# Retention and two MLPs on one core: conversion and retention steps dealt out in slots a step apart, and a pair's load moved behind the step that frees its place

## The chip, the cores and the metric

One core of a Trainium2 chip. TensorE multiplies, VectorE, ScalarE and GpSimd do element work, SP issues most of the DMAs. Each engine runs its own list in the order in which it was written and waits at semaphores. The metric is device time in microseconds of one execution.

## The reference

```python
scores = (q @ k.T) / sqrt(64)                      # 4 batches, 8 heads, 576 positions, 64 wide
ret    = scores * gamma[h] ** (i - j) * (j <= i)   # retention: decay, causal
x      = (ret @ v) -> 2304 tokens x 512
x      = softplus(x @ w_in1) @ w_out1              # d_ff 2048
out    = h * sigmoid(1.702 * h) @ w_out2, h = x @ w_in2
```

The weights come in as 64-bit words.

## The kernel before, in words

The 2304 tokens are worked in five blocks: 512 positions of each of the batches 0 to 3, and a block "t" with the last 64 positions of all four (256 tokens). `order` is 0, 1, 2, t, 3, first through layer 1, then through layer 2. A block has 16 units f, one for each 128 columns of d_ff. A unit is two halves on TensorE: `mm1` (12 matmuls into `ph`) and, two units behind (LAG), `mm2` (12 into the four banks `y`). Every product is made of three, since both operands are split into a high and a low part (`hi` casts, `lo` subtracts). Between the halves ScalarE turns `ph` into g, casts it to gh, and VectorE subtracts to gl (`start`, `split`; `split` runs as `hook` behind the first of mm2's four sub-products).

Everything else of layer 1 is dealt out between the products. `side()` is called twice in mm1 and twice in mm2; each call adds a rate to two counters and for each whole one takes a slot, which is one `next()` of a generator. Two generators are in it:

- `batch(b)`: the retention of the next batch, eight pair-chunks (two heads, 256 positions). `scale_pair` (ScalarE) and `load_pair` (SP, three places `raw`) in one slot, `step` in the next. A step puts out the chunk before (TensorE reads its q and v, so only then is its place free) and makes states `sv`, scores and masked scores `a` of the new one; VectorE does all that follows TensorE in it. Rate 0.31.
- the conversion of weights (`conv`): a tile of words goes through ScalarE (L92), three VectorE instructions (L94, L95, L98), a ScalarE cast and a VectorE subtraction (`lo`, L82), in four slots. In block 0 these are the 16 tiles of layer 1 (`w1_steps`, rate 1.25, and `pre` forces f + 2 tiles ahead of unit f). From block 1 on they are 32 half tiles of layer 2 (`w2_steps`, rate W2RATE), which are read by SP, converted, stored to HBM and loaded again in layer 2; words and results share two places (`raw64`), and what is left of them at block 3's start is done there at once.

Ahead of block 0, `first_batch` runs the first batch's retention alone, with two conversion slots behind each step from the sixth on. At a block's end `done` copies each y bank to one of two `yb` tiles and stores it. At a block's start `pre` empties the retention generator and splits the new x.

## Time and profile before

| what | us |
|---|---|
| time, median of 3 runs (lowest to highest) | 934.18 (933.38 to 937.91) |
| profiled execution | 934.67 |
| its span, first to last instruction | 933.0 |
| TensorE busy | 889.5 (95%) |
| VectorE busy | 407.4 (44%) |
| ScalarE busy | 302.9 (32%) |
| GpSimd busy | 20.3 (2%) |
| granted clock, mean | 0.979 |

Busy times are means over stages that differ. The span is the profiled execution's own; 1.67 us lie around it. PE is TensorE, PEld its weight loads, DVE VectorE, ACT ScalarE, POOL GpSimd, SPq the queue of SP. A releaser behind "<-" is what ended a wait. L82 and L79 / L77 are the lines of the helpers `lo` and `hi`, so their rows are told apart by the names of the tiles.

### The profile page before, as it was taken

What the parts mean: (1) busy time and instruction counts of PE and PEld (TensorE: products, weight loads), DVE (VectorE), ACT (ScalarE), POOL (GpSimd) and SP (SyncE); (2) the same over time, 40 slices, a digit from 0 to 9 for tenths busy, and PEclk for the clock granted to TensorE, in tenths of its full rate; (3) what the DMA queues carried; (4) which work ended last, traced back from release to release, by engine and by line L of the source; (5) the groups of instructions that cost most, each with busy time, mean ns of one, the idle gap of its engine ahead of it and who ended that gap; (6) DMA issues with size and microseconds to landing.
All of it is one profiled execution on the core that took longest, in us unless ns stands there. A gap on an engine that the chain in (4) does not pass through costs nothing.

```text
span 933.0 us, 12052 instructions
## 1 busy us (share of the span) xinstructions
PE 889.5 (95%) x4928; PEld 732.3 (78%) x4928; DVE 407.4 (44%) x759; ACT 302.9 (32%) x541; POOL 20.3 (2%) x41
## 2 busy tenths in 40 slices
PE   9588798999999999989999999999999999999997
PEld 5366577888887778879888888888888888988886
DVE  7877774366666566621211232232223222333222
ACT  3344343334444334422322322232223222333221
POOL 0000000000000000000100110000000000000000
PEclk9799789999999999999999999999999999999999
DMA  9804432245556655420355640001001000200001
GB/s 353 348 1 139 162 114 105 76 172 205 188 181 235 208 210 185 166 109 1 122 208 189 214 148 1 1 31 61 0 1 68 1 1 0 91 2 22 1 1 45
DMA packets 33783, 101.71 MB, mean 109 GB/s; under 512 B 3392, under 2 KB 5440, under 8 KB 31680
## 3 DMA queue, kind: packets, MB, share of 16 engines
q1 hardware_dynamic: 29952, 79.45, 24.1%
q0 software_dynamic: 3776, 21.50, 6.5%
q8 instruction: 38, 0.62, 0.3%
q14 instruction: 17, 0.14, 0.1%
HBM read 74.72 MB, written 26.21 MB: 108 GB/s over the span
## 4 chain that ended last, share of the span: by engine, by line
PE 72%; issue 13%; DVE 7%; DMA 5%; ACT 2%; SPq 0%; POOL 0%; DVEq 0%; ACTq 0%; POOLq 0%
PE ph L111 35%; PE y L111 34%; DMA w_raw<-w_in 2%; PE ps_h L273 2%; DVE wa L98 2%; DVE wa L95 1%; DMA w_kqv<-kqv 1%; DVE w_raw L94 1%; DMA w_raw<-w_out 1%; PE ps_s L304 1%; DVE a L317 1%; ACT wa L92 1%; DVE sv L312 1%; DVE w L82 1%; DMA raw<-kqv 1%
## 5 line engine op out<-in xcount | busy, mean ns | idle before, releaser
L111 PE MATMUL ph<-xh,w 128*128 128x512 f32 (+1 forms) x1280 | 372.6, 376 | 14.1 <-DVE xf L327 6.1
L111 PEld LDWEIGHTS ph<-xh,w 128*128 128x128 f32 x1280 | 236.0, 192 | 60.1 <-issue 6.9
L111 PE MATMUL ph<-xl,w 128*128 128x512 f32 (+1 forms) x640 | 239.7, 375 | 3.4 <-DVE xl L82 3.4
L111 PE MATMUL y<-gh,w 128*128 128x512 f32 (+1 forms) x640 | 198.7, 374 | 5.7 <-DVE yb L79 3.7
L111 PE MATMUL y<-w,gh 128*128 128x512 f32 x576 | 189.5, 389 | 0.0
L82 DVE TENSOR_TENSOR gl<-g,gh 128x512 fp32r<-128x512 f32 (+1 forms) x160 | 102.2, 639 | 183.9 <-ACT gh L77 181.6
L174 DVE TENSOR_TENSOR g<-ph,g 128x512 f32<-128x512 f32 (+1 forms) x80 | 51.0, 638 | 214.3 <-ACT g L167 214.3
L111 PEld LDWEIGHTS ph<-xl,w 128*128 128x128 f32 x640 | 123.2, 192 | 25.6 <-DVE xl L82 4.6
L111 PEld LDWEIGHTS y<-gh,w 128*128 128x128 f32 x640 | 118.6, 191 | 28.7 <-DVE yb L79 4.5
L111 PEld LDWEIGHTS y<-w,gh 128*128 128x128 f32 x576 | 108.1, 188 | 22.0
L111 PE MATMUL y<-gl,w 128*128 128x512 f32 (+1 forms) x320 | 118.6, 371 | 0.0
L167 ACT ACTIVATE g<-ph 128x512 f32<-128x512 f32 (+1 forms) x80 | 44.4, 555 | 224.7 <-PE ph L111 220.8
L111 PE MATMUL y<-w,gl 128*128 128x512 f32 x288 | 112.2, 390 | 0.0
L77 ACT CAST gh<-g 128x512 fp32r<-128x512 f32 (+1 forms) x160 | 92.5, 578 | 57.5 <-DVE g L174 55.1
L165 ACT ACTIVATE g<-ph 128x512 f32<-128x512 f32 (+1 forms) x80 | 43.8, 548 | 110.3 <-PE ph L111 110.3
L111 PEld LDWEIGHTS y<-gl,w 128*128 128x128 f32 x320 | 61.0, 191 | 9.8
L111 PEld LDWEIGHTS y<-w,gl 128*128 128x128 f32 x288 | 54.2, 188 | 10.7
L77 ACT CAST halves<-wa 128x512 fp32r<-128x512 f32 x32 | 19.9, 621 | 77.6 <-DVE wa L98 55.3
L92 ACT ACTIVATE wa<-raw 128x512 f32<-128x512 f32 x32 | 21.4, 670 | 46.2 <-DMA raw<-w_out 27.4
L82 DVE TENSOR_TENSOR halves<-wa,halves 128x512 fp32r<-128x512 f32 x32 | 22.1, 691 | 26.8 <-ACT halves L77 26.8
L77 ACT CAST w<-wa 128x1024 fp32r<-128x1024 f32 x16 | 16.8, 1048 | 47.8 <-DVE wa L98 47.8
L94 DVE TENSOR_SCALAR raw<-raw 128x512 uint32<-128x512 uint32 x32 | 13.7, 427 | 33.9 <-ACT wa L92 33.9
(83 smaller groups left out, 550.1 us busy)
## 6 DMA issues: line engine op xcount, KB each, us to landing
w2d<-halves SPq DMA_DIRECT2D x32, 512.0 KB, 3.5
w<-w2d POOLq DMA_DIRECT2D x16, 1024.0 KB, 5.1
raw<-kqv SPq DMA_DIRECT2D x24, 512.0 KB, 4.5
w_raw<-w_in SPq DMA_DIRECT2D x16, 512.0 KB, 8.4
w_raw<-w_out SPq DMA_DIRECT2D x16, 512.0 KB, 8.8
raw<-w_in SPq DMA_DIRECT2D x16, 512.0 KB, 3.5
raw<-w_out SPq DMA_DIRECT2D x16, 512.0 KB, 3.5
w_kqv<-kqv SPq DMA_DIRECT2D x8, 512.0 KB, 8.7
```

The source lines that it names most:

```text
L77: nc.scalar.copy(dst, src)
L82: nc.vector.tensor_tensor(out=dst, in0=src, in1=f32(h), op=ALU.subtract)
L92: nc.scalar.mul(a, high.bitcast(F32), 2.0 ** -112)
L94: nc.vector.tensor_single_scalar(out=high, in_=high, scalar=0x80000000, op=ALU.bitwise_and)
L95: nc.vector.scalar_tensor_tensor(out=u, in0=u, scalar=3, in1=high, op0=ALU.logical_shift_left, op1=ALU.bitwise_or)
L98: nc.vector.scalar_tensor_tensor(out=u, in0=low, scalar=29, in1=u, op0=ALU.logical_shift_right, op1=ALU.bitwise_or)
L111: nc.tensor.matmul(out_ap, l, r, start=first and i == 0, stop=last and i == k - 1)
L165: nc.scalar.activation(g, ph, AF.Softplus)
L167: nc.scalar.activation(g, ph, AF.Sigmoid, scale=1.702)
L174: nc.vector.tensor_tensor(out=g, in0=ph, in1=g, op=ALU.mult)
L273: nc.tensor.matmul(po[halves[h], at], l, rhs, start=clear[h], stop=True, skip_group_check=True)
L304: nc.tensor.matmul(ps[h][:, j], k[r, j], q[r, j], start=True, stop=True)
```

## The change

- `from_words`, `w1_steps` and the loop of `w2_steps` become one generator `convert`. Its slots for a tile: L94 and L95; L98; the cast and, right behind it, the next tile's L92; the subtraction. The read of a half tile of layer 2 (`begin`) comes a slot after the store (`end`) of the tile two before it.
- `split` leaves the subtraction gl to `rest`, called behind mm2's third sub-product.
- `step` becomes a generator with a yield between TensorE's part and what follows it. The first state copies of a pair go to ScalarE. In batches 0 and 1 the second head's masked scores are made by a ScalarE scaling and a GpSimd select.
- `load_pair` for pair i + 2 comes behind step i, which freed its place; three pairs are loaded at a batch's start.
- Rates: retention 0.31 to 0.52, layer 1's conversion 1.25 to 1.0, W2RATE 1.0 to 0.75; in `first_batch` one slot behind each step from the fifth on. One weight load stands a pair earlier. `yb` has three places.

```diff
@@ -21,7 +21,7 @@
 RB = 3
 WARM = 14
 FILL = 2
-W2RATE = 1.0
+W2RATE = 0.75
 @with_exitstack
@@ -82,21 +82,42 @@
         nc.vector.tensor_tensor(out=dst, in0=src, in1=f32(h), op=ALU.subtract)
-    def from_words(words, a):
...
+    def convert(n, ready, words, place, begin, end):
+        def rebase(i):
+            w = words(i)
+            a = wr.tile([P, 2 * DM], F32, tag="wa", name="wa")[:, 0:w.shape[1]]
+            nc.scalar.mul(a, w[:, :, 1].bitcast(F32), 2.0 ** -112)
+            return w, a
+        nxt = None
+        for i in range(n):
+            while nxt is None:
+                if ready(i):
+                    nxt = rebase(i)
+                yield
+            w, a = nxt
+            u = a.bitcast(U32)
+            low, high = w[:, :, 0], w[:, :, 1]
+            nc.vector.tensor_single_scalar(out=high, in_=high, scalar=0x80000000, op=ALU.bitwise_and)
+            nc.vector.scalar_tensor_tensor(
+                out=u, in0=u, scalar=3, in1=high, op0=ALU.logical_shift_left, op1=ALU.bitwise_or)
+            begin(i)
+            yield
+            nc.vector.scalar_tensor_tensor(
+                out=u, in0=low, scalar=29, in1=u, op0=ALU.logical_shift_right, op1=ALU.bitwise_or)
+            yield
+            h, l = place(i)
+            hi("a", h, a)
+            nxt = rebase(i + 1) if i + 1 < n and ready(i + 1) else None
+            yield
+            lo(l, a, h)
+            end(i)
+            yield
     def w_tile():
         return wp.tile([P, 2, 2, DM], F32R, tag="w", name="w")
@@ -150,7 +171,9 @@
                 if last:
                     done(layer, key, n, e, ys[key][e])
                 if e == 0:
-                    hook()
+                    rest = hook()
+                if e == min(2, cnt - 1):
+                    rest()
                 if e % 2 or e == cnt - 1:
                     side()
             if last:
@@ -173,8 +196,8 @@
             if it[0] == 2:
                 nc.vector.tensor_tensor(out=g, in0=ph, in1=g, op=ALU.mult)
             hi("a", gh, g)
-            lo(gl, g, gh)
             ts[it] = gh, gl
+            return lambda: lo(gl, g, gh)
         n_work = len(work)
         for i in range(n_work + LAG):
@@ -182,20 +205,19 @@
             if cur:
                 pre(*cur)
             if cur and cur[3] == 0 and i >= LAG:
-                mm2(work[i - LAG], lambda: None)
-                split(cur, *start(cur, mm1(cur)))
+                mm2(work[i - LAG], lambda: lambda: None)
+                split(cur, *start(cur, mm1(cur)))()
                 continue
             if cur:
                 g, ph = start(cur, mm1(cur))
             def hook():
-                if cur:
-                    split(cur, g, ph)
+                return split(cur, g, ph) if cur else lambda: None
             if i >= LAG:
                 mm2(work[i - LAG], hook)
             else:
-                hook()
+                hook()()
     with tc.manual_schedule():
         nc.scalar.preload_act_table_set("softplus")
@@ -262,11 +284,13 @@
                     y = x[:, :, halves[h]]
                     nc.scalar.mul(y, y, sdec[:, 2 * p + h:2 * p + h + 1])
-            def step(out_i, i, banks):
+            def step(out_i, i, banks, on_act, later):
                 po, ps = banks[0], banks[1:]
+                ends_at = slice(2 * C0 - D, 2 * C0)
+                cols = [slice(C0 + (t + 1) * D, C0 + (t + 2) * D) for t in range(2)]
                 clear = [True, True]
                 def put(h, at, l, rhs):
@@ -291,31 +315,41 @@
                 if i is not None:
                     b, c, p = pairs[i]
                     k, q, x, v, e = loaded[i]
-                    ends_at = slice(2 * C0 - D, 2 * C0)
                     if c:
                         for h, r in enumerate(halves):
                             put(h, ends_at, e[:, r], e[:, P:P + D])
-                    cols = [slice(C0 + (t + 1) * D, C0 + (t + 2) * D) for t in range(2)]
                     for t in range(2):
                         for h, r in enumerate(halves):
                             put(h, cols[t], x[:, t, r], v[:, t, r])
                     for j in (slice(0, P), slice(P, C0)):
                         for h, r in enumerate(halves):
                             nc.tensor.matmul(ps[h][:, j], k[r, j], q[r, j], start=True, stop=True)
+                if later:
+                    yield
+                if i is not None:
+                    b, c, p = pairs[i]
                     states = [None] + svs[p % 2] if c == 0 else svs[p % 2][1:]
                     for t in range(2):
                         for r in halves:
                             sv, new = states[t + 1][r, r], po[r, cols[t]]
                             if states[t] is None:
-                                hi("v", sv, new)
+                                hi("a", sv, new)
                             else:
                                 nc.vector.scalar_tensor_tensor(
                                     out=sv, in0=states[t][r, r], scalar=gdec[r, p:p + 1], in1=new,
                                     op0=ALU.mult, op1=ALU.add)
                     a = ap.tile([P, 2 * C0 + D], F32, tag="a", name="a", bufs=2)
                     for h in range(2):
+                        ah, rd = a[:, h * C0:(h + 1) * C0], rdec[:, 2 * p + h:2 * p + h + 1]
+                        if h and on_act:
+                            nc.scalar.mul(ah, ps[h][:, 0:C0], rd)
+                            ah = ah.rearrange("p (t j) -> p t j", t=2)
+                            nc.gpsimd.affine_select(
+                                out=ah, in_=ah, compare_op=ALU.is_ge, fill=0.0,
+                                base=0, pattern=[[0, 2], [1, P]], channel_multiplier=-1)
+                            continue
                         nc.vector.scalar_tensor_tensor(
-                            out=a[:, h * C0:(h + 1) * C0], in0=ps[h][:, 0:C0], scalar=rdec[:, 2 * p + h:2 * p + h + 1],
+                            out=ah, in0=ps[h][:, 0:C0], scalar=rd,
                             in1=mask[:, 0:4, :].rearrange("p t j -> p (t j)"), op0=ALU.mult, op1=ALU.mult)
                     if c:
                         nc.vector.scalar_tensor_tensor(
@@ -340,16 +374,18 @@
                 xf[b] = xf_tile()
                 i0, i1 = 2 * NPAIR * b, 2 * NPAIR * (b + 1)
-                for i in range(i0, i0 + RB - 1):
+                for i in range(i0, i0 + RB):
                     load_pair(i)
                 yield
                 for i in range(i0, i1 + 1):
                     if i < i1:
                         scale_pair(i)
-                        if i + RB - 1 < i1:
-                            load_pair(i + RB - 1)
                     yield
-                    step(i - 1 if i > i0 else None, i if i < i1 else None, [bank(ps_h, "h"), bank(ps_a, "s"), bank(ps_a, "o")])
+                    out_i = i - 1 if i > i0 else None
+                    banks = [bank(ps_h, "h"), bank(ps_a, "s"), bank(ps_a, "o")]
+                    yield from step(out_i, i if i < i1 else None, banks, b < 2, True)
+                    if out_i is not None and out_i + RB < i1:
+                        load_pair(out_i + RB)
                     yield
             def first_batch():
@@ -368,10 +404,10 @@
                 load(1)
                 nc.sync.dma_start(out=end, in_=ends[0])
                 nc.sync.dma_start(out=odec, in_=outdecay)
-                for i in range(2, 5):
+                for i in range(2, 4):
                     load(i)
                 w1_load(0)
-                for i in range(5, n):
+                for i in range(4, n):
                     load(i)
                 w1_load(1)
                 scale_pair(0)
@@ -383,7 +419,8 @@
                     while late:
                         late.pop()()
                     banks = [bank(ps_h, "h"), bank(ps_a, "s"), bank(ps_a, "o")] if i % 2 == 0 else [bank(ps_y, "y") for _ in range(3)]
-                    step(i - 2 if i >= 2 else None, i if i < n else None, banks)
+                    for _ in step(i - 2 if i >= 2 else None, i if i < n else None, banks, True, False):
+                        pass
                     if i >= 3 and i % 2:
                         late.append(split_x(0, 1, xf[0], i // 2 - 1))
                     for _ in range(FILL if i < n + 1 else 0):
@@ -427,35 +464,26 @@
                         nc.sync.dma_start(
                             out=words[:, s * 2 * DM:(s + 1) * 2 * DM], in_=w_src(w1_in, w1_out, f, s))
-            def w1_steps():
...
             made = {"f": 0}
-            w1_gen = w1_steps()
+            def w1_place(f):
+                w1[f] = w_tile()
+                return [w1[f][:, i].rearrange("p s n -> p (s n)") for i in range(2)]
+            w1_gen = convert(
+                NF, lambda f: (1, f) in raws, lambda f: raws.pop((1, f)), w1_place, lambda f: None,
+                lambda f: made.update(f=f + 1))
             x_tiles(order[0], 1)
             for i, _ in enumerate(first_batch()):
                 if i in (4, 7):
                     w1_load(i // 3 + 1)
-                if i >= 5:
+                if i >= 4:
                     next(w1_gen, None)
-                    next(w1_gen, None)
             side_gen = {"g": iter(()), "acc": 0.0, "rate": 0.0}
-            conv = {"g": w1_gen, "acc": 0.0, "rate": 1.25}
+            conv = {"g": w1_gen, "acc": 0.0, "rate": 1.0}
             def side():
                 for s in (side_gen, conv):
@@ -471,23 +499,24 @@
                         out=t.rearrange("p n two -> p (n two)"), in_=w_src(w2_in, w2_out, i // 2, i % 2))
                     raws[2, i] = t
+            w2_half = {}
+            def w2_place(i):
+                w2_half["t"] = wr.tile([P, 2, DM], F32R, tag="raw64", name="halves")
+                return w2_half["t"][:, 0], w2_half["t"][:, 1]
+            def w2_store(i):
+                nc.sync.dma_start(out=f32(w2d[i // 2][:, :, i % 2, :]), in_=f32(w2_half["t"]))
             def w2_steps():
                 w2_read(0)
                 w2_read(1)
                 for _ in range(8):
                     yield
-                for i in range(2 * NF):
...
+                yield from convert(
+                    2 * NF, lambda i: (2, i) in raws, lambda i: raws.pop((2, i)), w2_place,
+                    lambda i: w2_read(i + 1) if i else None, w2_store)
             w2_gen = w2_steps()
@@ -513,7 +542,7 @@
                             split_block(key, 1, xt if key == "t" else xf[key])
                         if i + 1 < B:
                             side_gen["g"] = batch(i + 1)
-                            side_gen["rate"] = 0.31
+                            side_gen["rate"] = 0.52
                         else:
                             side_gen["g"] = iter(())
                         if i == 1:
@@ -540,7 +569,7 @@
             def done(layer, key, n, e, y):
                 w = n if layer == 1 else DM
-                yb = tp.tile([P, T], F32, tag="yb", name="yb", bufs=2)[:, 0:w]
+                yb = tp.tile([P, T], F32, tag="yb", name="yb", bufs=3)[:, 0:w]
                 hi("v" if e % 2 else "a", yb, y[:, 0:w])
                 if layer == 1:
                     nc.gpsimd.dma_start(out=y1[key][e], in_=yb)
```

## Rows read from the trace of the kernel before

**Rows 1.** Stages: length, busy TensorE, weight loads, VectorE, ScalarE, GpSimd (instructions), clock, DMA.

```profile
0.00:54.54 54.54, 41.43 (x356) 27.16 (x357) 41.41 (x98) 20.75 (x34) 0.61 (x5) 0.87 0.77 300
54.54:175.03 120.49, 104.73 (x625) 82.54 (x624) 82.19 (x131) 47.13 (x71) 0.00 (x0) 0.92 0.32 111
175.03:280.69 105.66, 105.38 (x673) 85.59 (x672) 65.49 (x142) 43.93 (x82) 2.32 (x4) 1.00 0.48 170
280.69:392.18 111.49, 106.03 (x674) 85.70 (x672) 70.01 (x149) 44.94 (x87) 2.18 (x4) 1.00 0.60 204
392.18:445.86 53.68, 49.98 (x386) 48.64 (x385) 15.20 (x33) 18.10 (x44) 2.17 (x4) 0.97 0.16 60
445.86:933.00 487.14, 481.94 (x2222) 402.63 (x2220) 133.08 (x211) 128.06 (x227) 13.07 (x24) 1.00 0.17 58
```

**Rows 2.** The chain that ended last: start, length, what (block t, block 3).

```profile
440.26 1.44 PE y L111 x12
...
474.71 2.72 PE ph L111 x12
```

**Rows 3.** Waits from 37 to 175 us: total, times, longest.

```profile
ACT w L77 <- DVE wa L98: 47.1, 15, 6.3
DVE gl L82 <- ACT gh L77: 20.3, 11, 4.7
ACT wa L92 <- DMA w_raw<-w_out: 12.7, 3, 6.7
```

**Rows 4.** Timeline of TensorE: start, length, instruction, idle time before it and its releaser.

```profile
47.23 0.80 PE L111 MATMUL ph<-xl,w 128*128 128x512 f32 x1 [2.33 <-DVE xl L82]
...
116.09 1.19 PE L111 MATMUL ph<-xh,w 128*128 128x512 f32 x2 [4.23 <-DVE xf L327]
```

**Rows 5.** VectorE's instructions by line from 54.54 to 175.03: busy, mean ns, idle before.

```profile
L95 DVE SCALAR_TENSOR_TENSOR wa<-wa,w_raw 128x1024 uint32<-128x1024 uint32 x12 | 14.7, 1226 | 0.4
L98 DVE SCALAR_TENSOR_TENSOR wa<-w_raw,wa 128x1024 uint32<-128x1024 uint32 x12 | 14.7, 1223 | 0.3
L82 DVE TENSOR_TENSOR w<-wa,w 128x1024 fp32r<-128x1024 f32 x12 | 14.7, 1223 | 8.9 <-ACT w L77 8.9
...
L94 DVE TENSOR_SCALAR w_raw<-w_raw 128x1024 uint32<-128x1024 uint32 x12 | 8.3, 694 | 6.0 <-ACT wa L92 6.0
...
L317 DVE SCALAR_TENSOR_TENSOR a<-ps_o,dec,mask 128x256 f32<-128x256 f32 x8 | 3.8, 475 | 0.0
...
L79 DVE COPY sv<-ps_h 64x64 f32<-64x64 f32 x8 | 1.8, 220 | 0.4 <-PE ps_h L273 0.3
```

**Rows 6.** Waits of SP, which issues the loads: total, times, longest.

```profile
SPq L251 <- PE ps_h L273: 156.4, 16, 38.4
...
SPq L470 <- DMA w2d<-halves: 64.8, 20, 6.3
```

**Rows 7.** ScalarE's and GpSimd's instructions by line, whole span.

```profile
L411 POOL TENSOR_SCALAR_AFFINE_SELECT mask<-mask 128x256 f32<-128x256 f32 x1 | 0.4, 403 | 2.5 <-DVE mask L410 2.5
...
L77 ACT CAST xh<-xt 128x256 fp32r<-128x256 f32 x4 | 1.3, 402 | 0.0
...
L77 ACT CAST w<-wa 128x1024 fp32r<-128x1024 f32 x16 | 16.8, 1048 | 47.8 <-DVE wa L98 47.8
```

**Rows 8.** Timeline: a second-layer tile's first and last instruction.

```profile
387.50 0.66 ACT L92 ACTIVATE wa<-raw 128x512 f32<-128x512 f32 x1 [2.61 <-DMA raw<-w_out]
...
392.04 0.53 SPq L488 DMA_DIRECT2D w2d<-halves  x1
```

**Rows 9.** DMA issues of the page: KB each, median us from issue to landing.

```profile
raw<-w_out SPq DMA_DIRECT2D x16, 512.0 KB, 3.5
```

**Rows 10.** Timeline: waits for the copies of y, at block 2's start and at the end.

```profile
297.04 0.50 PE L111 MATMUL y<-gh,w 128*128 128x512 f32 x1 [1.99 <-DVE yb L79]
...
929.35 0.69 DVE L79 COPY yb<-y 128x512 f32<-128x512 f32 x1 [2.17 <-DMA out<-yb]
```

**Rows 11.** Waits, whole span: total, times, longest.

```profile
ACT wa L92 <- DMA raw<-w_out: 27.4, 15, 3.3
```

More of the change, by code (lines that the diff above doesn't have):

```diff
@@ L82, in lo @@
         nc.vector.tensor_tensor(out=dst, in0=src, in1=f32(h), op=ALU.subtract)
-    def from_words(words, a):
-        low, high = words[:, :, 0], words[:, :, 1]
-        u = a.bitcast(U32)
-        nc.scalar.mul(a, high.bitcast(F32), 2.0 ** -112)
-        yield
-        nc.vector.tensor_single_scalar(out=high, in_=high, scalar=0x80000000, op=ALU.bitwise_and)
-        nc.vector.scalar_tensor_tensor(
-            out=u, in0=u, scalar=3, in1=high, op0=ALU.logical_shift_left, op1=ALU.bitwise_or)
-        yield
-        nc.vector.scalar_tensor_tensor(
-            out=u, in0=low, scalar=29, in1=u, op0=ALU.logical_shift_right, op1=ALU.bitwise_or)
+    def convert(n, ready, words, place, begin, end):
[28 more added lines that the diff above has]
+            yield
     def w_tile():
@@ L428, in w1_load @@
                             out=words[:, s * 2 * DM:(s + 1) * 2 * DM], in_=w_src(w1_in, w1_out, f, s))
-            def w1_steps():
-                for f in range(NF):
-                    while (1, f) not in raws:
-                        yield
-                    a = wr.tile([P, 2 * DM], F32, tag="wa", name="wa")
-                    for _ in from_words(raws.pop((1, f)), a):
-                        yield
-                    w1[f] = w_tile()
-                    h, l = (w1[f][:, i].rearrange("p s n -> p (s n)") for i in range(2))
-                    hi("a", h, a)
-                    yield
-                    lo(l, a, h)
-                    made["f"] = f + 1
-                    yield
-            made = {"f": 0}
-            w1_gen = w1_steps()
+            made = {"f": 0}
+            def w1_place(f):
[4 more added lines that the diff above has]
+                lambda f: made.update(f=f + 1))
             x_tiles(order[0], 1)
@@ L479, in w2_steps @@
                     yield
-                for i in range(2 * NF):
-                    a = wr.tile([P, 2 * DM], F32, tag="wa", name="wa")[:, 0:DM]
-                    for _ in from_words(raws.pop((2, i)), a):
-                        yield
-                    t = wr.tile([P, 2, DM], F32R, tag="raw64", name="halves")
-                    hi("a", t[:, 0], a)
-                    yield
-                    lo(t[:, 1], a, t[:, 0])
-                    nc.sync.dma_start(out=f32(w2d[i // 2][:, :, i % 2, :]), in_=f32(t))
-                    w2_read(i + 2)
-                    yield
+                yield from convert(
+                    2 * NF, lambda i: (2, i) in raws, lambda i: raws.pop((2, i)), w2_place,
+                    lambda i: w2_read(i + 1) if i else None, w2_store)
             w2_gen = w2_steps()
```

## The prediction

> **What bounds the kernel now.** I read the views from the coarse to the fine: the stages, the pace of one product, then for the stages that fall behind the waits, the instructions of the engine they wait for, and the order on it. The stage table cuts the span at the first product of each block of tokens [rows 1]. The reader is to see that the last 487.14 us (block 3 of layer 1 and all of layer 2) have TensorE busy for all but 5.2 us at the full clock: twelve products of 512 columns take 2.72 us and follow each other without a hole [rows 2]. Nothing in the change can shorten them; they set a floor. Block 1 (105.66 us) holds 32 such halves, 87.04 us, and the retention of the next batch, so 18.6 us for a batch's retention with its transitions, and it is on the floor too: TensorE is busy for 105.38.
>
> What is over the floor lies in four places. From 54.54 to 175.03 block 0 runs 28 halves (28 x 12 of its 625 matmuls, nearly all others being retention): 28 x 2.72 + 18.6 = 94.8 us would do, it takes 120.49, so 25.7 us are lost, part of them at a mean granted clock of 0.92. Block 2 has block 1's work and takes 111.49, 5.8 more. The tail block "t" has 32 halves of 1.44 us [rows 2], one of them still 512 wide: 16 x 1.44 + 2.72 + 15 x 1.44 = 47.4; it takes 53.68, so 6.3 are lost. And the first 54.54 us hold the load of the first batch, its retention and three halves of block 0, with TensorE busy for 41.43 at a clock of 0.87.
>
> In block 0 the waits show three engines handing one conversion tile round [rows 3]: ScalarE waits 47.1 us for the shift-or at L98 that VectorE was given in the same slot, VectorE waits 20.3 for ScalarE's gh, and three times ScalarE waits for raw words (12.7 us). Each engine runs its own list in order, so TensorE gets what stands behind: it waited 4.23 us for xf, behind a cast, a subtraction and the step's own work on VectorE [rows 4]. The same ring at the start of block 0 held up the last xl, behind a tile's subtraction, for which TensorE waited 2.33 us at 47.23 [rows 4].
>
> **The change part by part.** *Conversion.* A tile costs VectorE 0.694 + 1.226 + 1.223 + 1.223 = 4.37 us [rows 5] before and after; no instruction goes. What goes is the handing round: the cast now comes a slot behind L98, the next tile's scaling right behind the cast, the subtraction a slot later. At one slot per call and four calls per product pair, block 0 makes one tile per pair, where 1.25 slots made it 1.25 tiles: VectorE's demand is spread over nearly all 16 pairs. Its work in block 0 is 82.19 us [rows 1]; less 8 copies of 0.22 and 8 masks of 0.475 (below) it is 76.6, in a floor of 94.8, 81% busy, where blocks 1 and 2 ran at 62% and 63%. So block 0 can come near its floor but not quite: I leave it a third of its loss, 8 of 25.7, and take 102.5, **-18**. Ends: floor 94.8 (-25.7), and -5 if only the waits for raw words go and 5 of their 12.7 us reached TensorE.
>
> *The load behind its step.* SP waited 156.4 us over 16 loads at L251 for the step that frees the pair's place, up to 38.4 us at a time [rows 6], and the weight loads behind it on the same queue landed late: that is the 12.7 us of [rows 3]. The moved load and its "ends" load find the place free; the three pairs loaded at a batch's start use three free places. A pair is then needed four slots on, 4 / 0.52 = 7.7 calls or 10.5 us, against 3.5 us in which a raw tile of the same 512 KB lands [rows 9]. Cost nothing; its gain is inside the -18.
>
> *gl two sub-products later.* VectorE no longer stands at gl until gh is there (20.3 us in [rows 3]). gl is used two pairs later, 10.9 us; moving it by two sub-products (1.4 us) costs nothing. The next g needs it read, 4 us on: covered while VectorE is less than that behind.
>
> *Copies and masks to ScalarE and GpSimd.* In the first batch and batch 1 the second half of the masked scores becomes a ScalarE scaling and a GpSimd select; in all batches the first state copies go to ScalarE. VectorE loses 16 x 0.475 and 32 x 0.22 us [rows 5]. The trace of before has one select of that shape, 0.403 us, and no ScalarE scaling of it out of PSUM; four casts of 128x256 took 0.402 each and a cast of 1024 columns 1.048 [rows 7]. Bounds: 0.26 (a quarter of the latter) to 1.05; I take 0.40, by the row of the same shape. 16 of them cost nothing, since ScalarE is busy for only 47.13 of block 0's 120.49 us; without that cover they are 6.4 us. New wait: VectorE's state update at c=0 now waits for ScalarE's copy; gl and the conversion are queued behind it. From 0 to one conversion cast on ScalarE (1.05) at each of 16 such steps; I take half, 8 us over four batches, on VectorE; block 0's quarter, 2 us, is in the 8 left to it, and the others meet a VectorE that has time.
> What speaks against the move is a rule: the Trainium skill, page "SBUF — State Buffer", section "Who interferes with whom", says that GpSimd shares a port pair with VectorE and that a VectorE instruction with two SBUF inputs and a GpSimd instruction that reads SBUF shut each other out for the whole instruction. No run here shows the two side by side; the only select stood alone. What it would do is rival (a).
>
> *Two halves of a step, rate 0.52.* Three slots at 0.52 per call: a batch takes 28 slots, 54 calls, 13.5 pairs, against 19 / 0.31 = 61 calls, 15.3 pairs. The bank of po is held two calls (2.7 us) longer; the product after next takes it 5.4 us later, so this is nearly covered. Bounds 0 to 1 us for a step in four, 0 to 6 us in all; I put 1 us each on blocks 1 and 2.
>
> *A third yb.* VectorE's copy of the last y waited for the store of the one two before it. TensorE lost 1.99 us to that at the start of block 2, and the kernel's last copy 2.17 [rows 10]; with three places the last one waits for the store one earlier, so 0.8 us go at the end. Block 2 gives back 5 of its 5.8 us by this and by the shorter rings, so with the 1 above **-4**, between -6 and 0. Block 1: **+1**, between 0 and +4.
>
> *Rate 0.75 for the second layer's weights.* Here I expect a loss. 96 slots fall into blocks 1 and 2; 8 are idle and one starts, so 21.75 of 32 tiles are done there, and 10.25 move to block t, where two were before. Raw words and halves share two places, so the read of tile i+2 waits for the store of tile i: SP stood at L470 for 64.8 us over 20 reads, 3.24 each [rows 6]. Then the words land in 3.5 [rows 9], and from scaling to store one tile took 392.04 - 387.50 = 4.5 us [rows 8]. So two tiles take 3.24 + 3.5 + 4.5 = 11.2 us at least, 5.6 a tile; at 0.75 a tile is scheduled every 5.33 calls, 3.84 us of block t (2.88 us a pair) but 7.3 and more in blocks 1 and 2. In block t ScalarE will stand at the scaling of each second tile with the next g behind it. Ten tiles: 10.25 x 5.6 = 57, of which the slack carried over from block 2 takes about 5, and then 2.5 pairs without conversion, 7 us: 59 to 61. I take 60.7, **+7**; ends +2 (a shorter chain) and +14 (every wait with g's and gl's own time in it).
>
> *Prologue.* The copies and masks of batch 0 (8 x 0.22 + 8 x 0.475 = 5.6 us) and the first two instructions of a third tile (1.9) leave VectorE's list ahead of the last xl, and the scaling of a pair no longer stands behind a cast. Against that, tiles 1 and 2 are made just in time, each 4.37 + 1.05 for the cast. The first y product moves from 54.5 to about 47.5: **-7**, between 0 and -11.
>
> **Sum.** -7 - 18 + 1 - 4 + 7 - 0.8 = -21.8. The profiled execution took 934.67 (span 933.0 and 1.67 around it), 0.49 above the median of 934.18: 934.67 - 21.8 = 912.9, about 912 beside the median.
>
> **Rivals.** (a) *The locks.* Each of the 16 selects keeps VectorE out for 0.403 us: 6.4 us of VectorE time, 3.2 in the prologue and 3.2 in block 0, both bound by it, against 7.6 saved. Price 5: 917. For it: the shift-ors and subtractions, 3 of the 4 instructions of a tile, read SBUF twice [rows 5]; against it: 0.4 us eight times is little beside the 19% of block 0 that VectorE would idle. (b) *VectorE is the bound of block 0.* 81%, in lumps of a whole step's work, may keep 18 of the 25.7: block 0 at 112.5, 10 more, 922. For it: the clock of 0.92 there, since stalls bring more; against it: block 2 at 63% loses little. (c) *Block 0 on its floor and the reads in time*: -25.7 and +2 in place of -18 and +7: 900. For it: the conversion's slots fall on the same calls of every pair. (d) *Slower: ScalarE is the new ring.* Its scaling waits for the words at the head of its list (27.4 us over 15 for one weight alone, 1.8 each [rows 11]), and now state copies stand behind it, and VectorE behind those. If 21 tiles in blocks 1 and 2 each pass 1.8 us to TensorE, that is +38 in place of -3: 953. It decides from 0.9 us a tile. Against it: the same waits cost block 1 nothing. (e) *The change doesn't do what it says*: the waits change hands; block 0 and the prologue give back 5 and 4, blocks 1 and 2 nothing, t takes 7: 934.67 - 9 + 7 - 0.8 = 932. For it: no instruction of the conversion goes; against it: two blocks of before with the same kinds of work show no loss.
>
> **Numbers.** Forecast 0.39; (a) 0.12, (b) 0.19, (c) 0.16, (d) 0.08, (e) 0.06. Half a per cent (4.7 us) is about what a measurement of this kernel tells from no change. Faster than 929.5: the first four less 0.03 for their slow ends, 0.83; within: 0.06 + 0.03 = 0.09; slower than 938.9: 0.08. Range 895 to 931: below it the low side of (c), above it (d) and part of (e).
>
> **What would show it.** Right: block 0 from its first y product to block 1 in 98 to 108 us with a granted clock near 1.00; ScalarE's wait for L98 far below 47 us; SP's wait at L251's successor a few us in all; block t at 58 to 65 us with ScalarE waiting for raw words in it; layer 2 unchanged. Wrong: block t at 54 or less (the chain of store and read is not what I think), selects followed by VectorE holes of 0.4 us, or block 0 above 112 with VectorE over 90% busy.

## The result, and the profile after

The median is 913.0 us (911.13 to 914.12 over 4 runs) against 935.78 us (933.38 to 937.91) of the kernel before beside it: a ratio of 0.9755, 95% interval [0.9722, 0.9789]. The profiled execution took 914.12 us, 20.55 less than that of before.

Stages of the kernel after, cut as in [rows 1] and with the same columns:

```profile
0.00:48.12 48.12, 38.94 (x368) 25.84 (x372) 35.97 (x81) 24.20 (x51) 4.27 (x13) 0.96 0.87 340
48.12:145.93 97.81, 95.25 (x610) 77.47 (x609) 77.43 (x115) 53.39 (x89) 3.51 (x8) 0.98 0.39 136
145.93:250.97 105.04, 105.04 (x673) 85.67 (x672) 52.91 (x115) 39.98 (x80) 2.31 (x4) 1.00 0.40 142
250.97:356.01 105.04, 105.04 (x673) 85.67 (x672) 60.81 (x130) 42.96 (x88) 2.16 (x4) 1.00 0.49 165
356.01:425.44 69.43, 55.08 (x385) 52.95 (x384) 33.36 (x62) 26.49 (x57) 2.16 (x4) 0.88 0.48 167
425.44:912.09 486.65, 481.95 (x2222) 402.64 (x2220) 133.72 (x211) 128.02 (x227) 13.02 (x24) 1.00 0.17 58
```

The prologue gave 6.4 us, block 0 22.7, block 1 0.6, block 2 6.5, the end 0.5; block t cost 15.75. Blocks 1 and 2 now have TensorE busy without a hole. Block 0 comes within 3 us of the 94.8 that the prediction gave as its floor. Block t is the one stage that got worse, by a lower clock (0.88) and by 14.35 us without a matmul where before had 3.70.

Waits of the kernel after: 37 to 146 us first (as [rows 3]), then SP's over the whole span (as [rows 6]), then block t:

```profile
ACT w L77 <- DVE wa L111: 22.8, 13, 4.0
DVE gl L82 <- ACT gh L77: 7.5, 2, 4.7
...
SPq L273 <- PE ps_h L297: 105.4, 12, 28.1
...
SPq L498 <- DMA w2d<-halves: 59.7, 22, 4.3
...
ACT wa L94 <- DMA raw<-w_out: 16.3, 5, 4.8
...
PE ph L132 <- ACT g L188: 8.4, 5, 3.4
...
PE y L132 <- DVE yb L79: 4.3, 1, 4.3
```

L111 is L98 of before: ScalarE's wait for it halved, and its wait for raw words of layer 1 is gone. SP still stands 105.4 us at the pair's load (L273, L251 before). In block t ScalarE waits for raw words of layer 2, with g behind it, and TensorE for g.

The entry into block t, from the timeline of the kernel after (start, length, instruction, idle before it and its releaser):

```profile
359.63 0.62 ACT L77 CAST halves<-wa 128x512 fp32r<-128x512 f32 x1 [1.17 <-DMA w2d<-halves]
...
363.33 0.66 ACT L94 ACTIVATE wa<-raw 128x512 f32<-128x512 f32 x1 [3.08 <-DMA raw<-w_out]
363.89 0.37 ACT L188 ACTIVATE g<-ph 128x256 f32<-128x256 f32 x1
364.16 0.58 ACT L77 COPY yb<-y 128x512 f32<-128x512 f32 x1
...
369.72 0.69 DVE L79 COPY yb<-y 128x512 f32<-128x512 f32 x1 [4.22 <-DMA y<-yb]
...
370.47 0.58 PE L132 MATMUL y<-gh,w 128*128 128x256 f32 x1 [4.26 <-DVE yb L79]
...
372.23 0.62 ACT L77 CAST halves<-wa 128x512 fp32r<-128x512 f32 x1 [5.82 <-DVE wa L111]
...
383.53 0.62 ACT L77 CAST halves<-wa 128x512 fp32r<-128x512 f32 x1 [1.45 <-DVE wa L111]
...
410.29 0.62 ACT L77 CAST halves<-wa 128x512 fp32r<-128x512 f32 x1 [1.23 <-DVE wa L111]
...
418.50 0.62 ACT L77 CAST halves<-wa 128x512 fp32r<-128x512 f32 x1 [1.45 <-DVE wa L111]
```

One scaling waits 3.08 us for its words. Behind it stand g and the copy of the last y; that store then starts late, the next y's copy waits 4.22 us for its place, and TensorE 4.26. The second of the ten casts waits 5.82 us, since L111 stands behind that copy in VectorE's list. From the first cast to the last 58.87 us pass, 6.54 a tile, but not evenly: the first three tiles take 23.90 us, the next five (383.53 to 410.29) 5.35 each, the last 8.21.

The kernel's last copy of y (as [rows 10]) waits 1.48 us where it waited 2.17:

```profile
908.24 0.69 DVE L79 COPY yb<-y 128x512 f32<-128x512 f32 x1 [1.48 <-DMA out<-yb]
```

### The profile page after: what moved, and what is told of

It reads as the page before. It is cut to its first block, busy times and chain, and to the rows that moved or that the text cites. A ratio compares the mean times of both kernels' runs of the same rounds, so it can differ in the third digit from the quotient of the medians.

```text
span 912.1 us, 12125 instructions
## 1 busy us (share of the span) xinstructions
PE 881.3 (97%) x4924; PEld 730.2 (80%) x4928; DVE 394.2 (43%) x711; ACT 315.0 (35%) x589; POOL 27.4 (3%) x57
## 4 chain that ended last, share of the span: by engine, by line
PE 74%; issue 12%; DMA 6%; DVE 5%; ACT 2%; SPq 0%; POOL 0%; DVEq 0%; ACTq 0%; POOLq 0%
PE ph L132 35%; PE y L132 35%; PE ps_h L297 2%; DMA raw<-w_out 2%; DMA w2d<-halves 2%; PE ps_s L326 1%; DVE wa L107 1%; DVE wa L111 1%; DMA w_end<-ends 1%; ACT wa L94 1%; DVE sv L338 1%; DMA w_raw<-w_in 1%; DMA y<-yb 0%; DMA raw<-w_in 0%; DVE halves L82 0%
## 5 line engine op out<-in xcount | busy, mean ns | idle before, releaser
L132 PE MATMUL ph<-xl,w 128*128 128x512 f32 (+1 forms) x640 | 237.2, 371 | 0.5 <-DVE xl L82 0.5
L132 PE MATMUL y<-gh,w 128*128 128x512 f32 (+1 forms) x640 | 200.8, 378 | 5.8 <-DVE yb L79 4.3
L132 PEld LDWEIGHTS y<-gh,w 128*128 128x128 f32 x640 | 120.9, 195 | 27.8 <-DVE yb L79 4.5
L338 DVE SCALAR_TENSOR_TENSOR sv<-sv,dec,ps_h 64x64 f32<-64x64 f32 x80 | 22.3, 279 | 39.8 <-ACT sv L77 36.6
L94 ACT ACTIVATE wa<-raw 128x512 f32<-128x512 f32 x32 | 21.4, 668 | 35.2 <-DMA raw<-w_out 25.4
L77 ACT CAST w<-wa 128x1024 fp32r<-128x1024 f32 x16 | 16.7, 1046 | 22.8 <-DVE wa L111 22.8
```

The source lines that it names most:

```text
L77: nc.scalar.copy(dst, src)
L94: nc.scalar.mul(a, w[:, :, 1].bitcast(F32), 2.0 ** -112)
L132: nc.tensor.matmul(out_ap, l, r, start=first and i == 0, stop=last and i == k - 1)
L338: nc.vector.scalar_tensor_tensor(out=sv, in0=states[t][r, r], scalar=gdec[r, p:p + 1], in1=new, op0=ALU.mult, op1=ALU.add)
```

## Experiments

Every run was timed together with the kernel before, and its ratio is to that kernel beside it (medians of 935.61 to 936.25 us); the line of before in the table is of its own three runs. Stage lengths come from each kernel's profile, cut as above; block 1's start is prologue and block 0 together. They are one profile each: in after, rate1, three_places, three_rate1 and best_pool, which do the same up to there but for a smaller warming tile in the last three, block 1 starts at 145.71 to 147.12, so differences of about 1.4 us there say nothing.

| kernel | median us | ratio to before [95%] | block 1 starts | block 1 | block 2 | t |
|---|---|---|---|---|---|---|
| before | 934.18 | | 175.03 | 105.66 | 111.49 | 53.68 |
| after | 913.0 | 0.9755 [0.9722, 0.9789] | 145.93 | 105.04 | 105.04 | 69.43 |
| rate1 | 907.2 | 0.9689 [0.967, 0.9709] | 145.71 | 105.04 | 111.22 | 55.01 |
| three_places | 903.8 | 0.9653 [0.9631, 0.9674] | 147.07 | 105.04 | 105.04 | 59.55 |
| ring | 908.59 | 0.9709 [0.969, 0.9729] | 144.58 | 105.04 | 105.76 | 63.52 |
| load_ahead | 915.81 | 0.9795 [0.9765, 0.9826] | 147.06 | 108.97 | 106.12 | 69.85 |
| rate125 | 930.25 | 0.9948 [0.9922, 0.9974] | 164.91 | 105.04 | 105.18 | 68.55 |
| ring_rate125 | 925.49 | 0.9887 [0.9851, 0.9922] | 161.86 | 105.04 | 105.56 | 63.21 |
| all_v | 912.95 | 0.9756 [0.9722, 0.9791] | 146.14 | 105.04 | 105.04 | 68.06 |
| three_rate1 | 904.15 | 0.9659 [0.9626, 0.9692] | 147.12 | 105.04 | 110.83 | 53.77 |
| before_rate1 | 917.24 | 0.9793 [0.976, 0.9826] | 154.82 | 106.37 | 110.89 | 53.57 |
| whole_gl | 915.56 | 0.9773 [0.9745, 0.9801] | 142.10 | 106.02 | 107.72 | 72.61 |
| best_ring | 892.3 | 0.9527 [0.9503, 0.955] | 145.35 | 105.04 | 105.91 | 47.51 |
| best_pool | 894.31 | 0.9542 [0.9516, 0.9569] | 146.94 | 105.04 | 105.14 | 48.47 |

**rate1: the second layer's rate put back.**

```diff
-W2RATE = 0.75
+W2RATE = 1.0
```

> The kernel after with W2RATE back at 1.0, so 29.75 of the 32 half tiles are converted in blocks 1 and 2 and 2.25 instead of 10.25 in block t. Theory (block t is held up by the chain store, read, scaling of the shared places): block t falls from 69.4 us to 52 to 56, blocks 1 and 2 stay within 2 us of 105.0 each, time about 899. Rival 1 (block t is slow since VectorE and ScalarE have too much other work there, whatever the places): same result for block t, so this run does not tell it apart; three_places does. Rival 2 (the words then come late in blocks 1 and 2 too, three calls = 4.1 us after the store in place of 5.4, and ScalarE passes that on): blocks 1 and 2 grow by 5 or more each, time 905 to 915.

Block t falls from 69.43 to 55.01, so the lower rate is its cause. Block 2 goes back up from 105.04 to 111.22, though yb has three places here too. So the time is 907.2 and not the 899 expected, in the range of rival 2, though block 1 did not grow. That extra time begins in one place; its stage and timeline:

```profile
250.75:361.96 111.21, 106.63 (x673) 86.85 (x672) 69.74 (x144) 47.13 (x95) 2.26 (x4) 0.98 0.57 194
```

```profile
255.98 0.62 ACT L77 CAST halves<-wa 128x512 fp32r<-128x512 f32 x1 [4.27 <-DMA w2d<-halves]
...
258.38 0.66 ACT L94 ACTIVATE wa<-raw 128x512 f32<-128x512 f32 x1 [1.78 <-DMA raw<-w_out]
...
259.57 0.53 PE L297 MATMUL ps_h<-raw 128*64 128x64 f32 x8 [4.58 <-ACT g L188]
```

A cast waits for the place that a store still reads, the next scaling for its words; g stands behind both, and TensorE loses 4.58 us of the stage's 4.6 us of idle time. The rest of the 6.2 us is TensorE's own time, at a clock of 0.98.

**three_places: three places for the words and halves of layer 2.** Room is made for it by a smaller tile for the warming products.

```diff
-t = wr.tile([P, DM, 2], U32, tag="raw64", name="raw64")
+t = wr.tile([P, DM, 2], U32, tag="raw64", name="raw64", bufs=3)
-w2_half["t"] = wr.tile([P, 2, DM], F32R, tag="raw64", name="halves")
+w2_half["t"] = wr.tile([P, 2, DM], F32R, tag="raw64", name="halves", bufs=3)
-warm_at["x"] = ac.tile([P, T], mybir.dt.bfloat16, name="warm")
+warm_at["x"] = ac.tile([P, 1, P], mybir.dt.bfloat16, name="warm")
-nc.tensor.matmul(warm_at["y"], x[:, 0:P], x, start=True, stop=True)
+nc.tensor.matmul(warm_at["y"], x[:, 0, :], x.to_broadcast([P, T // P, P]), start=True, stop=True)
```

> The kernel after with three places for words and halves in place of two, all rates as they are (to make room, the warm-up matmuls read a 128-column tile four times instead of one of 512 columns). A read no longer waits for the store just before it. Theory: block t falls from 69.4 to 50 to 55 us with the same 10.25 tiles in it, ScalarE's waits for the words in block t go from 21 us to under 6, time about 897. Rival (VectorE and ScalarE are simply too busy in block t: 33.4 and 26.5 us of work in 46 us of products, in lumps): block t stays above 62 and the time above 906.

Its block t, and ScalarE's wait for words of w_out in it:

```profile
357.15:416.70 59.55, 52.26 (x385) 50.65 (x384) 32.53 (x61) 25.84 (x56) 2.16 (x4) 0.91 0.59 195
```

```profile
ACT wa L94 <- DMA raw<-w_out: 13.4, 5, 3.7
```

One more place takes 9.9 of the 15.75 us off block t with the rate as it is. So the two places are the larger part of the loss. The expectation was met in part: block t is above its 50 to 55 us, and ScalarE's waits for words (16.3 and 4.5 us in after) fell to 13.4 and 0.7 only, not under 6. SP no longer waits for a store to land in block t, but its reads stand behind stores that wait 30.6 us for VectorE's subtraction. What is left, 5.9 us, was not split further.

**ring: the cast back in L111's slot, the scaling in a slot of its own.**

```diff
             nc.vector.scalar_tensor_tensor(   # L111
-            yield
             h, l = place(i)
             hi("a", h, a)
-            nxt = rebase(i + 1) if ... else None
             yield
             lo(l, a, h)
             end(i)
             yield
+            nxt = rebase(i + 1) if ... else None
+            yield
```

> The kernel after, but a tile's slots dealt as before: scaling; L106 and L107; L111 and the cast in one slot; the subtraction. Rates, slots per tile and everything else as after. Theory 1 (what block 0 gained, 21.7 us, comes from handing round a slot later): block 0 grows from 98.8 to 108 or more, ScalarE's wait for L111 goes back from 23 us to over 35, time 922 or more. Theory 2 (it comes from the lower rate, which spreads VectorE's work): block 0 within 3 us of 98.8, time 911 to 917.

Theory 2 holds in the main: block 0 does not grow (94.68 us; the 98.8 of the expectation was cut a microsecond earlier and is 97.81 here), though ScalarE's wait for L111 does. Block 1 starts 1.4 us earlier than in after, which is within the spread of such starts, so the new order gains nothing in block 0. The time is below the expected range because block t is 5.9 us shorter (63.52): there the new order is a loss. At the entry of block t TensorE's holes before y products are 0.6 us in place of 6.0.

**rate125 and ring_rate125: layer 1's conversion at 1.25 slots again, alone and with ring's order.**

```diff
-conv = {"g": w1_gen, "acc": 0.0, "rate": 1.0}
+conv = {"g": w1_gen, "acc": 0.0, "rate": 1.25}
```

> The kernel after with the conversion of layer 1 at 1.25 slots a call again in block 0 (everything else as after). The run that dealt the slots as before left block 0 as fast as after (block 1 began at 144.6 us against 145.9), so the handing round is not what block 0 gained from. Theory A (the rate: 1.25 tiles a pair ask more of VectorE than a pair lasts): block 1 begins 8 us later or more, at 154 to 170 us, time 920 or more. Theory B (masks and state copies off VectorE, or the retention in three slots, did it): block 1 begins within 3 us of 145.9, time 911 to 917.

> The kernel after with both the old dealing of a tile's slots and 1.25 slots a call in block 0. Theory A1 (the rate alone): as rate125, within 3 us. Theory A2 (the handing round costs when VectorE is behind, and only then): slower than rate125 by 5 us or more in block 0. Theory B: block 1 begins within 3 us of 145.9.

**before_rate1: the kernel before with that one number changed.**

```diff
-conv = {"g": w1_gen, "acc": 0.0, "rate": 1.25}
+conv = {"g": w1_gen, "acc": 0.0, "rate": 1.0}
```

> The kernel before with one number changed: layer 1's conversion at 1.0 slots a call in place of 1.25. Theory A (the rate is what block 0 gained from): block 1 begins at 155 to 162 us in place of 175.0, the rest as before, time 915 to 923. Rival (the rate helps only with the slots dealt out anew, masks and copies moved or the load behind its step): block 1 begins at 168 or later, time 929 or more.

These four go together. Block 0 in ring, before_rate1 and rate125; then ScalarE's wait for the shift-or between 37 and 165 us in the same three:

```profile
49.90:144.58 94.68, 93.53 (x610) 76.27 (x609) 77.72 (x115) 53.71 (x89) 5.28 (x8) 1.00 0.40 141
```

```profile
54.96:154.82 99.86, 96.85 (x625) 76.95 (x624) 80.12 (x130) 46.79 (x71) 0.00 (x0) 1.00 0.38 134
```

```profile
51.30:164.91 113.61, 102.23 (x611) 81.97 (x610) 77.28 (x115) 51.19 (x87) 4.09 (x8) 0.92 0.33 117
```

```profile
ACT w L77 <- DVE wa L111: 37.3, 15, 4.0
```

```profile
ACT w L77 <- DVE wa L98: 47.9, 15, 5.2
```

```profile
ACT w L77 <- DVE wa L111: 47.0, 15, 5.1
```

The rate alone, in before, makes block 0 20.6 us shorter (120.49 to 99.86) and starts block 1 20.2 us earlier (175.03 to 154.82), with the handing round untouched: ScalarE waits 47.9 us, as it did. The new order alone, at the old rate, keeps ScalarE at 47.0 us and starts block 1 at 164.91. And with the old order at the new rate ScalarE waits 37.3 us in place of 22.8, and block 1 starts no later than in after; at 1.25 the old order is 3 us ahead, at the edge of what A1 allowed and against A2. ScalarE's wait for VectorE is no measure of what TensorE loses.

What the rate does shows in two stretches of 20 us of rate125 and two of after (columns as [rows 1]):

```profile
70.00:90.00 20.00, 20.00 (x142) 16.32 (x141) 18.24 (x28) 12.82 (x21) 1.39 (x2) 1.00 0.44 162
90.00:110.00 20.00, 16.29 (x92) 12.99 (x91) 15.08 (x24) 9.33 (x16) 1.07 (x2) 0.83 0.38 139
```

```profile
88.00:108.00 20.00, 20.00 (x142) 16.31 (x142) 17.42 (x28) 11.53 (x20) 0.82 (x2) 1.00 0.54 200
108.00:128.00 20.00, 20.00 (x143) 16.30 (x142) 17.43 (x27) 11.79 (x20) 0.81 (x2) 1.00 0.34 114
```

VectorE has the same 77.3 and 77.4 us of work in block 0 of both. At 1.25 it is busy for 18.24 of 20 us at first, and in the stretch behind TensorE idles for 3.7 us, with a mean granted clock of 0.83, between its levels of 2.4 GHz (1.00) and 1.2; at 1.0 it is even, 17.4 and 17.4. They are examples: after has one hole above 0.5 us in block 0 (2.13, at 70.75), rate125 six. Four of the six (7.0 of 11.38 us) end with a g or a pair's scaling that stood in ScalarE's list behind a cast waiting for L111, one (2.0) with xf at the end of a full VectorE list, and one (2.3) with a g behind a scaling that waits for words. The first of them:

```profile
62.93 1.04 ACT L77 CAST w<-wa 128x1024 fp32r<-128x1024 f32 x1 [4.33 <-DVE wa L111]
...
64.92 0.58 ACT L188 ACTIVATE g<-ph 128x512 f32<-128x512 f32 x1
...
65.55 0.82 PE L132 MATMUL ph<-xh,w 128*128 128x512 f32 x2 [1.91 <-ACT g L188]
```

In before six of nine holes (8.3 of 15.8 us) stand behind such a cast, three behind VectorE's own list, none behind a wait for words. So the loss does reach TensorE through the handing round; what took it away is the rate, in either order. Why is in part open: at 1.0 a tile's four slots also fall on the same four calls of every pair, while at 1.25 they move from pair to pair, and no run separates this fixed place from the lower demand on VectorE.

Over block 0 rate125 loses 15.8 us against after: 8.8 of idle TensorE (11.38 against 2.56) and 7.0 in longer matmuls at the clock that came with it.

**load_ahead: the pair's load ahead of the step again.** Two pairs are loaded at a batch's start, pair i + 2 behind the scaling of pair i.

```diff
-for i in range(i0, i0 + RB):
+for i in range(i0, i0 + RB - 1):
...
 scale_pair(i)
+if i + RB - 1 < i1:
+    load_pair(i + RB - 1)
...
-if out_i is not None and out_i + RB < i1:
-    load_pair(out_i + RB)
```

> The kernel after with the load of a pair back ahead of the step that frees its place (two pairs at a batch's start). Theory: SP stands at the load for over 130 us again, the weights' words behind it land late, block 0 grows by 3 to 8 us, blocks 1 and 2 by less than 2, time 916 to 923. Rival (the words have time enough at the lower rate): block 0 within 1.5 us, time 912 to 915.

Its blocks 0 and 1, and SP's wait:

```profile
49.39:147.06 97.67, 95.12 (x611) 77.47 (x610) 77.42 (x115) 53.34 (x89) 3.50 (x8) 0.98 0.42 147
147.06:256.02 108.96, 107.17 (x673) 87.09 (x672) 52.79 (x114) 39.70 (x80) 2.32 (x4) 0.98 0.41 136
```

```profile
SPq L273 <- PE ps_h L297: 141.2, 17, 28.9
```

SP waits 36 us longer and block 0 is the same. In this profile block 1 is 3.9 us longer and block 2 1.1; the medians differ by 2.8 us, but the intervals of the two ratios overlap and this run's profiled execution (920.48 us, the others 914.42 to 915.82) is the far one. The load's place is worth nothing in block 0; no gain behind it is shown.

**all_v: state copies and masks back on VectorE** (no scaling on ScalarE, no select).

```diff
-hi("a", sv, new)
+hi("v", sv, new)
-yield from step(out_i, i if i < i1 else None, banks, b < 2, True)
+yield from step(out_i, i if i < i1 else None, banks, False, True)
-for _ in step(i - 2 if i >= 2 else None, i if i < n else None, banks, True, False):
+for _ in step(i - 2 if i >= 2 else None, i if i < n else None, banks, False, False):
```

> The kernel after with the masked scores and the state copies back on VectorE in every batch, so without GpSimd selects and ScalarE scalings of scores. Theory B1 (their 5.6 us in the prologue and 5.6 in block 0 are part of the gain): block 1 begins 4 to 12 us later than 145.9, time 917 to 925. Rival (VectorE has room for them at the lower rate, or the selects cost what they save): block 1 begins within 2 us of 145.9, time 911 to 915.

Prologue and block 0:

```profile
0.00:50.96 50.96, 42.80 (x372) 27.38 (x372) 40.70 (x97) 19.97 (x36) 0.61 (x5) 0.93 0.83 321
50.96:146.14 95.18, 93.53 (x611) 76.28 (x609) 81.87 (x131) 48.70 (x73) 0.00 (x0) 1.00 0.40 140
```

The move to ScalarE and GpSimd is worth 0 here: 912.95 against 913.0. The first y product comes 2.8 us later without it, and block 0 is 2.6 shorter. With 4.4 us more work, VectorE is 86% busy in block 0, and TensorE's granted clock is 1.00 there.

**whole_gl: a step in one slot at rate 0.31, and gl at once.**

```diff
-if e == min(2, cnt - 1):
+if e == 0:
     rest()
-yield from step(out_i, i if i < i1 else None, banks, b < 2, True)
+yield from step(out_i, i if i < i1 else None, banks, b < 2, False)
-side_gen["rate"] = 0.52
+side_gen["rate"] = 0.31
```

> The kernel after with a step again in one slot at rate 0.31 and gl again at once behind gh (the load stays behind its step). Theory C (the 10 us that the rate leaves over in the prologue and block 0 are theirs): block 1 begins 4 to 12 us later than 145.9, time 917 to 925. Rival (they only fit the new slots): within 2 us, time 911 to 915.

```profile
47.49:142.10 94.61, 94.61 (x625) 76.76 (x624) 78.38 (x117) 54.17 (x89) 5.33 (x8) 1.00 0.34 119
```

Block 0 is on its floor, TensorE busy for all of it, and block 1 starts 3.8 us earlier; blocks 1, 2 and t then give back 1.0, 2.7 and 3.2. The two edits, taken together, move time between stages; the total is 2.6 us above that of after, with overlapping intervals, so no gain or loss of theirs is shown.

**three_rate1, best_ring, best_pool: towards a faster kernel.** All have three places and W2RATE 1.0; best_ring adds the order of ring, best_pool has the words' reads on GpSimd's queue:

```diff
-                    nc.sync.dma_start(
+                    nc.gpsimd.dma_start(
```

> The kernel after with three places for words and halves and W2RATE 1.0 (warm-up matmuls read a 128-column tile four times). Theory: with 2.25 tiles left block t takes 49 to 53 us, and the cast at the start of block 2, which with two places waited 4.3 us for a store, finds a place, so block 2 is back at 105 to 106.5: time 893 to 897. Rival (the late start of block 2 at rate 1.0 has to do with the rate itself, the stores of block 1 and the words on one set of DMA rings): block 2 at 109 or more, time 898 to 903.

> The kernel after with W2RATE 1.0, three places for words and halves (warm-up matmuls on a 128-column tile) and the old dealing of a tile's slots, in which the next scaling comes three slots behind the read instead of two and ScalarE stands less at the words with g behind it. Theory: block 2 back at 105 to 107 (110.8 without the old dealing), block t 50 to 53: time 893 to 898. Rival (the words are late at a block's start because their read stands behind a store that waits for VectorE, whatever the slot): block 2 at 109 or more, time 901 to 905.

> The kernel after with W2RATE 1.0, three places (warm-up matmuls on a 128-column tile) and the reads of layer 2's words issued by GpSimd instead of SP, where they stood behind a store that waits for VectorE's subtraction. Theory (that order on SP is what makes the words late at a block's start): block 2 at 105 to 107, block t 49 to 53, time 893 to 898. Rival (GpSimd's own stores of y at the block's start hold the reads up instead, or its issue is slower): block 2 at 109 or more, time 901 or more.

Three places and rate 1.0 do not add up: block t is 53.77, but block 2 is 110.83, as the rival of three_rate1 had it. Its timeline:

```profile
256.12 0.62 ACT L77 CAST halves<-wa 128x512 fp32r<-128x512 f32 x1 [2.80 <-DVE wa L111]
...
259.47 0.66 ACT L94 ACTIVATE wa<-raw 128x512 f32<-128x512 f32 x1 [2.73 <-DMA raw<-w_out]
```

The wait for a place is gone, but the cast now waits for L111 and the scaling still for its words. Two different edits cure it: ring's order (105.91), and reads on GpSimd's queue, where no store of halves stands ahead of them (105.14). Block 2 and block t of best_ring:

```profile
250.39:356.29 105.90, 105.12 (x673) 85.67 (x672) 69.85 (x145) 46.38 (x94) 2.18 (x4) 1.00 0.65 215
356.29:403.81 47.52, 47.52 (x386) 46.94 (x385) 12.81 (x27) 17.27 (x41) 2.17 (x4) 1.00 0.16 57
```

Block t is on the 47.4 us that its products need, with no hole. best_ring, 892.3 us, is the fastest version, 0.9527 [0.9503, 0.955] of before; best_pool's interval overlaps it.

## Why the prediction was right, and where it was not

The forecast of 912 us and its range hold, and the sign of all the large terms. Part of the exactness is luck: blocks 0 to 2 gave 8.8 us more than forecast (4.7, 1.6 and 2.5), and block t took 8.75 more.

- *Block 0, -18 predicted, -22.7 measured.* Of the two reasons given, the spreading of VectorE's demand at the lower rate was right as to the rate: it makes block 0 20.6 us shorter alone in before and 15.8 longer when undone in after. That the even spreading is what the rate does was not separated from the fixed place of its slots. "What goes is the handing round", by the order of the slots, was wrong: the order gains nothing in block 0, and most holes that the rate took away had come through that very handing round. VectorE ended 79% busy, as the 81% said; that a third of the loss would stay was too careful, since even at 86% (all_v) nothing was lost.
- *Prologue, -7 predicted, -6.4 measured.* Copies and masks gone from VectorE's list are 2.8 of it by all_v, but are given back in block 0. The rest was not separated.
- *The load behind its step.* "Its gain is inside the -18" failed: load_ahead has the same block 0. The 12.7 us for words, put down to SP's queue, also vanish in before_rate1, where the load is where it was; rate125, with the load moved, still has 4.0 of them. No hole of block 0 in before stood behind them. "SP's wait a few us" failed too: SP runs ahead of the step and stands 105.4 us, at no cost that a run shows.
- *Copies and masks.* The scaling out of PSUM, taken at 0.40 us, took 0.472 (12 of them) and 0.462 (4). VectorE's new wait for ScalarE's state copies, taken at 8 us in all and 2 in block 0, came to 36.6 and 6.2. It cost no time that the runs show: all_v has none of it and takes as long.
- *gl later and the step in two.* Priced at +1 in block 1 and +1 in block 2; measured by whole_gl they cost 3.8 us up to the start of block 1 and save 1.0, 2.7 and 3.2 behind it. Which of the two does which was not tried.
- *Block 2, -4 predicted, -6.5 measured, for a reason that was half right.* In before one hole of 1.99 us was the wait for yb, as said; it is gone in rate1, which has the third yb. The other three (3.5 us) end with a g behind a scaling that waits for words of layer 2, a wait that the -4 did not name. In rate1 this loss is back as one meeting of a cast, a scaling and g (4.58 us). It does not occur at the rate of 0.75 (105.04), nor at 1.0 with three places and the old order (105.91).
- *Block t, +7 predicted, +15.75 measured, beyond the end of +14.* The step was the right one, the count too (10.25 tiles predicted, ten there), and its price of 5.6 us a tile fits the five tiles in the middle (5.35). What the +7 left out is the entry, where the scaling holds up g and the copy of y (TensorE's holes before y products are 6.0 us, 3.7 in before), and the clock of 0.88, by which TensorE was busy 5.1 us longer (55.08 against 49.98). The entry is the work of the new order: ring, with the old one, has 0.6 there and block t at 63.52, +9.8.
- *The end, -0.8 predicted, -0.5 measured.*
- *Rivals.* (a) fell: the selects cost VectorE 0.16 us in all (last section), not 6.4, and where they met it, they were the ones that waited. (b) fell: block 0 took 97.81, not 112.5. (c) came half true, block 0 near the floor with the reads not in time. (d)'s place was wrong (blocks 1 and 2 hold 105.04), its mechanism is what block t and rate1's block 2 show: a scaling at the head of ScalarE's list, with g behind it. (e) fell.

## What to carry to other kernels

Work given out between products has a rate, and the rate comes first: the same instructions at 1.0 slots a call instead of 1.25 were worth 16 to 21 of the 23 us in block 0 here, while the finer order within a tile gained nothing there and cost 5.9 us in block t. A long wait between two side engines, or of a queue that runs ahead, says nothing until an instruction that TensorE needs stands behind it. Work pushed out of one stage lands in the next: count there how many places its load and store share, and what else stands in the list of the engine that waits for it.

## What the hardware showed that was not expected

The 16 selects have a median of 408 ns, as the one of before (403). Beside 14 of them VectorE runs nothing but state updates, masks and outputs that read PSUM, in their usual lengths. Two meet the conversion. Timeline of the kernel after:

```profile
21.30 0.68 DVE L106 TENSOR_SCALAR w_raw<-w_raw 128x1024 uint32<-128x1024 uint32 x1
21.44 0.81 POOL L347 TENSOR_SCALAR_AFFINE_SELECT a<-a 128x256 f32<-128x256 f32 x1 [0.54 <-DVE xf L361]
...
22.02 1.30 DVE L107 SCALAR_TENSOR_TENSOR wa<-wa,w_raw 128x1024 uint32<-128x1024 uint32 x1
```

The select begun beside L106 took 0.81 us (0.65 at 63.28) and ended 0.27 us after L106 both times; the shift-or behind L106 took 1.305 in place of 1.226. By the Trainium skill, page "SBUF — State Buffer", section "Who interferes with whom", the engine that comes second to the shared ports stands until the first has done; that the selects end so soon after L106 agrees. The price to VectorE was 0.08 us, twice, where rival (a) had put 0.403 sixteen times. In ring more of them meet the conversion, and there too the select is the one that waits, while the subtraction beside it keeps its length (1.21 to 1.23 us in all 16 of them):

```profile
83.88 1.23 DVE L82 TENSOR_TENSOR w<-wa,w 128x1024 fp32r<-128x1024 f32 x1 [0.52 <-ACT w L77]
84.29 1.08 POOL L347 TENSOR_SCALAR_AFFINE_SELECT a<-a 128x256 f32<-128x256 f32 x1 [6.39 <-ACT a L345]
```

Of the 16 selects in ring four begin beside such a subtraction and take 1.08 to 1.36 us, with block 0 at its floor (94.68): the longer selects cost nothing there.
